# Order of work at the front of an adaLN block, and one VectorE operation moved between two others

## The chip, the cores and the metric

The kernel runs on one core of a Trainium2 chip. The metric is the device time of one execution in microseconds (us), as the median of several runs. The engines of the core have short names: PE is TensorE, DVE is VectorE, ACT is ScalarE, POOL is GpSimd, and SP issues most of the fetches. Each engine has an instruction stream of its own, written out in the order of the program, and waits for the others by semaphores.

## The reference

One transformer-like block works on x of 2048 tokens by 448 channels. A vector c gives six rows of 448 by silu(c) @ w_mod: shift, scale and gate of two halves.

```python
mod = (silu(c) @ w_mod)               # sa, ca, ga, sb, cb, gb
h = layernorm(x) * (1 + ca) + sa
x = x + ga * A(h)                     # linear attention, 16 heads of 28
h = layernorm(x) * (1 + cb) + sb
x = x + gb * B(h)                     # token-mixing MLP, 2048 -> 1792 -> 2048 over tokens

def A(h):
    q, k, v = split_heads(h @ wqkv)
    pq, pk = phi(q), phi(k)           # phi(t) = (t + 1 if t > 0 else exp(t)) + 1e-6
    kv, z = sum_s pk * v, sum_s pk
    return ((pq @ kv) / (pq @ z + 1e-6)) @ wo

def B(h):
    return (gelu(layernorm(h).T @ w1 + b1) @ w2 + b2).T
```

All data are 32-bit floats.

## The kernel before

Tokens are worked on in 16 tiles of 128. The 448 channels are cut in four chunks of 128, 128, 128 and 64. To keep the accuracy, an operand of a matrix product is split into a high part (a rounded copy that ACT writes) and a low part (the rest, which DVE or POOL writes as operand minus high part); three products of high and low parts take the place of one. Names follow that: `hh`, `hl` are the high and low parts of x transposed, `wh`, `wl` those of a projection, `pth`, `ptl` those of phi(q) transposed. The fourth chunk has 64 rows, and its low part is put into partitions 64 to 127 of the same tile as the high part.

**The front.** The projection Wk (`raw_w[1, ch]`, shown as `wr`) is scaled row by row with 1 + ca. That scale is computed in place: `col_sum(1, ch)` on DVE (line 222) multiplies a chunk of w_mod (`wt`) with a row that PE has spread over all partitions (`scr`), sums along the row, and leaves a column. Then `w_high` on ACT (line 264) scales the chunk of Wk and rounds it, and `w_low` on DVE (line 276) writes the rest. `col_sum(0, ch)` does the same for the shift sa, from which `row_part`, `row_sum` and `row_bias` make a bias row. The mean of the first layernorm is taken off after the projection: the statistics of a pair of tiles (mean and the two roots of the variance, made by `a_pow` on POOL, line 356) are written as columns of a small tile by `a_rows` (a cast, line 399, and a low part, line 402), transposed by PE (`a_transpose`, line 408), copied by ACT (`a_copy`, line 411) into spare rows of `hl`, and `close` (line 443) adds mean times column sum and bias over root in one more matmul, whose other operand is `wrow`, written by `row_out` (an ACT copy and a DVE low part, line 299). The statistics come from ACT for tiles 0 and 1 and from DVE for the others (`a_stats_dve`: `first` is BATCH_NORM_STATS, line 384, `second` the aggregate, line 387, `end` the addition of epsilon and the power on POOL). Transposed x comes as its own array (`load_xt`), already laid out on the host; SP fetches it (line 131) and the chunks of w_mod (line 142) and Wk (line 149) in the order of the program.

`projects(seq, ...)` issues the matmuls of k = h Wk (`kp`, line 436) in a list's order; `in_turn(t)` is the usual list of ten for a tile t. From tile 4 on, a loop does for each tile the projection, the closing matmul, phi(k), and the outer product of phi(k) with normalised x (`a_outer`, line 548).

**The middle** (b stage). A loop of 16 + 5 steps i works as a pipeline over tiles. In step i PE transposes the scaled phi(q) of tile i (`b_transpose`, line 848, result `tq`), multiplies the one of tile i - 1 with the joint matrix of kv and wo (`b_out`, line 878, and `b_out_last`, line 885, for the fourth chunk), computes q for a coming tile and adds the contribution of tile i - 5 to the MLP's first product (`step`, lines 935 to 937). DVE, in the order of the program, adds the residual (`b_res`, line 894), makes the denominator of tile i + 1, normalises, writes the low part of tile i (`b_low`, line 863), takes the reciprocal of the denominator (`b_recip`, line 831), writes the low parts of the fourth chunks (`b_low_last`, line 870) and scales phi(q) of tile i + 1 (`b_scale`, line 835, result `pn`); then comes the low part of the normalised tile i - 4 (`b_low2`, line 932, `h2l`). The fourth chunks of tiles i - 1 and i are transposed together when i is odd, so `b_low_last` writes two tiles then and nothing when i is even. One of its two operations reads partitions 64 to 127 and writes 0 to 63, the other does the reverse.

After that stage the MLP's two products follow, the second by a fast scheme of seven products for eight. The change doesn't touch them.

The order of instructions on every engine is the order in which the Python program calls these functions; nothing reorders them. The tiles' places in memory are given out from pools in that order too.

Of the kernel before, what the change touches and what calls it, by code (L numbers as in the profile page):

```python
# [8 lines left out]
F32 = mybir.dt.float32  # L9
# [5 lines left out]
P = 128  # L15
# [37 lines left out]
def block_kernel(ctx: ExitStack, tc: tile.TileContext, x, xt, wqkv, wo, w1, b1, w2, b2, c, wmod, wfirst, out):  # L53
# [75 lines left out]
    def load_xt(t):  # L129
        XT[t] = slot(f"xt{t}", 512)  # L130
        nc.sync.dma_start(XT[t], xt[t])
# [24 lines left out]
    for ch in range(1, 4):  # L156
        load_first(1, ch)
        load_qkv(1, chs=(ch,))
        if ch == 1:
            load_xt(1)  # L160
    load_xt(2)
    load_x(0)
    for ch in range(4):
# [53 lines left out]
    def col_sum(j, ch):  # L217
        if j not in col:
            col[j] = cst.tile([P, 4], F32, name=f"col{j}")
        p = slice(0, 64 if j == 0 and ch == 3 else P)  # L220
        w = wt.pop((j, ch))[p]
        nc.vector.scalar_tensor_tensor(w, w, 1.0, scr[p, :D + 1], op0=ALU.mult, op1=ALU.mult,
                                       accum_out=col[j][p, ch:ch + 1])
# [38 lines left out]
    def w_high(j, ch):  # L262
        Whi[j, ch] = moving(tslot, f"wh{j}_{ch}")
        nc.scalar.activation(Whi[j, ch], raw_w[j, ch], AF.Identity, scale=col[1][:, ch:ch + 1])
# [5 lines left out]
    def w_low(j, ch):  # L270
        w, r = Whi[j, ch], raw_w[j, ch]
        p = slice(0, P) if ch < 3 else slice(64, P)
        if ch < 3:
            Wlo[j, ch] = moving(tslot, f"wl{j}_{ch}")
        out = Wlo[j, ch] if ch < 3 else w[p]
        nc.vector.scalar_tensor_tensor(out, r[p], col[1][p, ch:ch + 1], w[p].bitcast(F32),
                                       op0=ALU.mult, op1=ALU.subtract)
# [119 lines left out]
    def a_rows(t):  # L397
        g, r = groups.pop(t)[:, :, 0:2], rowst[t // 2 % RING].rearrange("p (t b c) -> p t b c", t=2, b=2)
        nc.vector.tensor_copy(r[:, :, :, 0:2], g.unsqueeze(2).to_broadcast([P, 2, 2, 2]))

        def low():
            nc.vector.tensor_sub(r[:, :, 0, 2:4], g, r[:, :, 0, 0:2].bitcast(F32))
        return low
# [9 lines left out]
    def a_split_high(t):  # L413
        heads[t] = (slot(f"hh{t}", 512, F32R), slot(f"hl{t}", 512, F32R))
        nc.scalar.activation(heads[t][0], XT[t], AF.Copy)
# [12 lines left out]
    def projects(seq, j, name):  # L428
        for t, kind, ch in seq:
            hh, hl = heads[t]  # L430
            first = (t, j) not in pps
            if first:
                pps[t, j] = bank(f"{name}{t}")
            w = Wlo[j, ch] if kind == "wl" else Whi[j, ch]
            a = hl if kind == "hl" else hh
            nc.tensor.matmul(pps[t, j][:, :D], a[:, ch * P:(ch + 1) * P], w, start=first, stop=False)  # L436
# [102 lines left out]
    def a_outer(t):  # L539
# [10 lines left out]
        if t < 2:  # L550
            for ch in range(4):
# [8 lines left out]
    w_high(1, 0)  # L560
    w_low(1, 0)
    w_high(1, 1)
    a_split_high(1)
    col_sum(1, 2)
    w_low(1, 1)
    w_high(1, 2)
    col_sum(1, 3)
    w_low(1, 2)
    w_high(1, 3)
    a_split_low(1)  # L570
    w_low(1, 3)
    a_split(2)
    projects([(0, "hh", 0), (0, "hl", 0), (0, "wl", 0), (0, "hh", 1), (0, "hl", 1), (1, "hh", 0), (1, "wl", 0),
              (1, "hh", 1), (0, "wl", 1), (1, "wl", 1), (0, "hh", 2), (0, "hl", 2), (1, "hh", 2), (0, "wl", 2),
              (1, "wl", 2), (1, "hl", 0), (1, "hl", 1), (1, "hl", 2), (0, "hh", 3), (1, "hh", 3)], 1, "kp")

    def in_turn(t):
        return [(t, kind, ch) for ch in range(3) for kind in ("hh", "wl")] + [(t, "hh", 3)] + \
# [17 lines left out]
    projects(in_turn(3)[4:], 1, "kp")  # L596
    a_split_high(4)
    a_split_high(5)
    low = a_rows(0)
    first23, second23, end23 = a_stats_dve((2, 3))  # L600
    first23(0)
    low()
    first23(1)
    second23(0)
    second23(1)
    end23()
    row_out(1)
    a_split_low(4)
    a_transpose(0)
    a_copy(0)  # L610
    a_copy(1)
    a_norm(0)
    a_split_low(5)
    projects(in_turn(4)[:3], 1, "kp")
    kps = [close(t, 1) for t in (0, 1)]
    projects(in_turn(4)[3:], 1, "kp")
    load_xt(9)
    load_x(9)
    load_mod(2)
# [6 lines left out]
    low()  # L626
    a_pk(0, kps[0])
    a_low(0)
    a_transpose(2)
    projects(in_turn(5), 1, "kp")  # L630
    first45, second45, end45 = a_stats_dve((4, 5))
    first45(0)
    first45(1)
# [228 lines left out]
        hi, lo = phs[t]  # L862
        nc.vector.tensor_sub(lo, tps[t][:, :384], hi[:, :384].bitcast(F32))

    def b_low_last(t):
        ps = tps.pop(t)
        if t % 2:
            for i, s, o in ((t - 1, slice(64, P), slice(0, 64)), (t, slice(0, 64), slice(64, P))):
                hi = phs[i][0]
                nc.vector.tensor_sub(hi[o, 384:], ps[s, 384:], hi[s, 384:].bitcast(F32))  # L870

    def b_out(t):
        ph, pl = phs[t]
# [98 lines left out]
    for i in range(NT + LAG):  # L972
        if i == NT - 4:
            load_mod(5)
        if NT - 3 <= i <= NT:
            mod_part(5, i - NT + 3)
        if i == NT:
            mod_split(5)
        if i % 2 == 0 and 0 < i <= NT:
            b_out_last(i - 2)  # L980
        if i < NT:
            b_transpose(i)
        if 0 <= i - 1 < NT:
            b_out(i - 1)
        nq = min(len(late), QS.get(i, 1))
        for _ in range(nq):
            a_q(late.pop(0))
        t = i - LAG
        if t >= 0:
            if t == 0:  # L990
                accs = [bank(f"up{f}") for f in range(4)]
            if i > NT:
                if not early:
                    early = [bank(f"up{W1G[1][0] + f}") for f in range(W1G[1][1])]
                r = i - NT - 1
                step(W1G[1][0], r, early, H2h[r], H2l[r])
            step(0, t, accs, H2h[t], H2l[t])
        if i == NT:
            mp = mod_sum2(5)
            mod_out(5, mp)  # L1000
        if i < NT:
            b_high(i)
            if i % 2 == 0:
                b_beside(i)
        a_exp_q(nq)
        scale, res, norm1, norm2 = i + 1 < NT, 0 <= i - 2 < NT, 0 <= i - 3 < NT, 0 <= i - 4 < NT
        if res and i < NT + 1:
            b_res(i - 2)
        if scale:
            b_prod(i + 1)  # L1010
        if norm2:
            b_norm2(i - 4, i)
        if res:
            b_mean1(i - 2, i)
        if norm1:
            b_norm1_a(i - 3)
        if scale:
            b_sum(i + 1)
        if norm1:
            b_norm1_b(i - 3, i)  # L1020
        if scale:
            b_eps(i + 1)
        if i < NT:
            b_low(i)
        if norm1:
            b_mean2(i - 3, i)
        split_end()
        if scale:
            b_recip(i + 1)
        if i < NT:  # L1030
            b_low_last(i)
        if scale:
            b_scale(i + 1)
        if i == NT:
            b_res(i - 1)
        if norm2:
            b_low2(i - 4)
        if i == 0:
            for ch in range(4):
                wp_split(ch)  # L1040
        a_phi_q(nq)
        load_to(max(14 + (i + 1) // 2, 12 + max(0, i - 6) + max(0, i - 14)))
        if res or norm1:
            b_rstd(i, 0 if res else 1, 2 if norm1 else 1)
        split_to(8 + max(0, i - 5))
# [315 lines left out]
```

## Time and profile before

| | us |
|---|---|
| median of 3 runs | 435.99 (435.96 to 436.09) |
| the profiled execution | 435.97 |
| its span, first to last instruction | 434.3 |
| PE busy | 428.0 |
| DVE busy | 362.4 |
| ACT busy | 278.7 |
| POOL busy | 118.6 |

The profile's page gives busy times, groups of instructions and waits of one execution. A row of the timeline has the start in us from the span's start, the duration in us, the engine, the line of the kernel, the operation, what is written and read, the shape, and in brackets how long the engine stood idle before it and what ended that. A matmul's busy time is modelled and overlaps its neighbours, so the distance from one start to the next is the better measure of PE's pace; undisturbed, that distance is 0.20 us for a matmul of 448 columns here.

### The profile page before, as it was taken

To read this page: it belongs to the slowest core of one execution; us is meant where nothing else is said; L and a number is where in the kernel's file an instruction comes from. 1 tells how busy PE (TensorE), PEld (TensorE's weight loads), DVE (VectorE), ACT (ScalarE), POOL (GpSimd) and SP (SyncE) were. 2 spreads that over 40 slices of the span, in tenths; PEclk is the share of its full clock that TensorE was granted. 3 is DMA by queue.
4 is the path that set the end of the run, shared out by engine and by line. 5 is a ranking of instruction groups with operands and counts; after the bars stand their busy time and mean duration, and the time that the engine had idled before them with its cause. 6 is when DMAs were issued, how large, how long until landed. Compare 5 with 4: busy or idle time off the path is not lost.

```text
span 434.3 us, 7208 instructions
## 1 busy us (share of the span) xinstructions
PE 428.0 (99%) x2333; PEld 395.3 (91%) x2333; DVE 362.4 (83%) x813; ACT 278.7 (64%) x595; POOL 118.6 (27%) x198
## 2 busy tenths in 40 slices
PE   8999999999999999999999999999999999999996
PEld 7688899999799989989999999999999999999996
DVE  4899987689799999996679695739798998898893
ACT  5799868658568799985855273537464664645550
POOL 4335443200025477765200000010113131132010
PEclk9999999999999999999999999999999999999999
DMA  8998996564300036345427461587469987885430
GB/s 285 383 331 166 241 248 160 108 222 167 87 1 0 26 72 149 73 97 122 146 85 230 154 211 50 163 211 203 84 183 213 205 181 153 215 183 118 82 54 32
DMA packets 63941, 66.14 MB, mean 152 GB/s; under 512 B 4960, under 2 KB 55456, under 8 KB 63904
## 3 DMA queue, kind: packets, MB, share of 16 engines
q1 hardware_dynamic: 54832, 50.90, 37.5%
q0 software_dynamic: 8784, 14.32, 20.9%
q10 hardware_dynamic: 288, 0.46, 0.4%
q8 instruction: 18, 0.29, 0.3%
q14 instruction: 19, 0.16, 0.1%
HBM read 46.30 MB, written 7.34 MB: 124 GB/s over the span
## 4 chain that ended last, share of the span: by engine, by line
PE 92%; DVE 4%; DMA 2%; issue 1%; POOL 0%; ACT 0%; SPq 0%; DVEq 0%
PE y L1156 19%; PE up L935 10%; PE up L937 10%; PE up L936 10%; PE y L1157 9%; PE cacc L548 8%; PE qp L436 7%; PE op L878 6%; PE kp L436 5%; PE tq L848 1%; PE op L885 1%; DMA wr<-in_qkv_dram 1%; PE kp L443 1%; DMA xt<-in_xt_dram 1%; PE qp L443 1%; PE kvb L802 1%
## 5 line engine op out<-in xcount | busy, mean ns | idle before, releaser
L935 PE MATMUL up<-h2h,ph 128*128 128x448 f32 x224 | 81.3, 363 | 0.0
L937 PE MATMUL up<-h2h,pl 128*128 128x448 f32 x224 | 81.2, 362 | 0.0
L936 PE MATMUL up<-h2l,ph 128*128 128x448 f32 x224 | 80.8, 361 | 0.0
L1111 POOL DMA_DIRECT2D a<-a x16 | 14.1, 953 | 138.7 <-DMA a<-in_B_w_dram 77.5
L937 PEld LDWEIGHTS up<-h2h,pl 128*128 128x128 f32 x224 | 42.0, 188 | 3.2
L936 PEld LDWEIGHTS up<-h2l,ph 128*128 128x128 f32 x224 | 41.9, 187 | 3.2 <-DVE h2l L932 0.3
L935 PEld LDWEIGHTS up<-h2h,ph 128*128 128x128 f32 x224 | 42.0, 188 | 2.2
L85 DVE TENSOR_TENSOR pl<-pr,ph 128x512 fp32r<-128x512 f32 x46 | 30.8, 687 | 4.1 <-ACT ph L84 3.3
L1162 ACT ACTIVATE cc<-y 128x448 f32<-128x448 f32 x24 | 13.0, 545 | 26.9 <-PE y L1157 26.9
L84 ACT ACTIVATE ph<-pr 128x512 fp32r<-128x512 f32 x46 | 27.6, 622 | 0.8 <-PE up L937 0.5
L1075 DVE TENSOR_TENSOR u<-u,mod 128x448 f32<-128x448 f32 x14 | 8.7, 622 | 21.7 <-ACT u L1074 21.5
L1074 ACT ACTIVATE u<-up,b1c 128x448 f32<-128x448 f32 x14 | 8.7, 624 | 24.1 <-PE up L937 23.5
L436 PE MATMUL kp<-wh,hh 128*128 128x448 f32 x64 | 24.0, 380 | 0.0
L548 PE MATMUL cacc<-pkh,xh 128*128 128x448 f32 x64 | 23.6, 369 | 0.0
L1176 POOL DMA_DIRECT2D out_dram<-yt x14 | 12.7, 908 | 39.9 <-DVE yt L1167 30.6
L436 PE MATMUL qp<-wh,hh 128*128 128x448 f32 x64 | 23.4, 366 | 0.0
L828 POOL TENSOR_SCALAR den<-den 128x16 f32<-128x16 f32 x16 | 8.8, 548 | 45.3 <-DVE den L825 45.3
L548 PE MATMUL cacc<-pkl,xh 128*128 128x448 f32 x56 | 20.3, 362 | 0.0
L878 PE MATMUL op<-wph,pth 128*128 128x448 f32 x48 | 18.7, 389 | 0.0
L1117 DVE TENSOR_TENSOR a<-a,s 128x512 f32<-128x512 f32 (+1 forms) x32 | 18.5, 619 | 0.0
L84 ACT ACTIVATE s2h<-s 128x512 fp32r<-128x512 f32 (+1 forms) x16 | 8.3, 569 | 15.5 <-DVE s L1117 15.5
L1156 PE MATMUL y<-ub,a11h 128*128 128x448 f32 x56 | 18.2, 375 | 0.0
(239 smaller groups left out, 1376.4 us busy)
## 6 DMA issues: line engine op xcount, KB each, us to landing
pr<-in_B_w_dram SPq DMA_DIRECT2D x56, 256.0 KB, 3.0
a<-in_B_w_dram SPq DMA_DIRECT2D x32, 256.0 KB, 4.5
a<-in_B_w_dram SPq DMA_DIRECT2D x32, 192.0 KB, 4.5
xt<-in_xt_dram SPq DMA_DIRECT2D x16, 256.0 KB, 5.0
x<-in_A_x_dram SPq DMA_DIRECT2D x16, 224.0 KB, 5.0
wm<-in_B_wmod_dram SPq DMA_DIRECT2D x16, 196.0 KB, 5.0
out_dram<-x SPq DMA_DIRECT2D x14, 224.0 KB, 2.2
out_dram<-yt POOLq DMA_DIRECT2D x14, 224.0 KB, 5.4
```

The source lines that it names most:

```text
L84: nc.scalar.activation(hi, full, AF.Copy)
L85: nc.vector.tensor_sub(lo, full, hi.bitcast(F32))
L436: nc.tensor.matmul(pps[t, j][:, :D], a[:, ch * P:(ch + 1) * P], w, start=first, stop=False)
L548: nc.tensor.matmul(cacc[ch][:, :D], a[:, s], b, start=(t == 0 and i == 0), stop=(t == NT - 1 and i == len(todo) - 1))
L878: nc.tensor.matmul(opb[t][:, :D], a, b, start=(ch == n == 0), stop=False)
L935: nc.tensor.matmul(ps[:, :D], hi[:, sl], mh, start=first, stop=False)
L936: nc.tensor.matmul(ps[:, :D], hi[:, sl], ml, start=False, stop=False)
L937: nc.tensor.matmul(ps[:, :D], lo[:, sl], mh, start=False, stop=last)
L1111: nc.gpsimd.dma_start(w, a, accum_op=ALU.add)
L1117: nc.vector.tensor_tensor(w, raw2[q, a][i], raw2[q, b][i], op=op)
L1156: nc.tensor.matmul(ps[:, :D], h[:, s], w, start=opens and r == 0, stop=False, skip_group_check=True)
L1157: nc.tensor.matmul(ps[:, :HD], l[:, s], wh, start=False, stop=closes and r == PAIRS - 1, skip_group_check=True)
```

## The change

It has five edits.

1. The fetch of transposed x of tile 1 is issued behind chunks 2 and 3 of the scale's weights and of Wk, instead of ahead of them.
2. In the preparation of Wk, the low part of chunk 1 goes ahead of the column sum of chunk 2, the low part of chunk 2 ahead of the column sum of chunk 3, and the high part of tile 1 follows chunk 2's high part. PE's list for tiles 0 and 1 is reordered: tile 0 by chunks (high-high, low of x, low of W), then tile 1.
3. The statistics of tile 2 go ahead of the rows of tiles 0 and 1; the low parts of these rows and `row_out(1)` go ahead of the statistics of tile 3.
4. On PE, one more matmul of tile 4 goes ahead of the closing matmuls of tiles 0 and 1, and three matmuls of tile 5 ahead of the second transpose of rows.
5. In odd steps of the b stage, `b_low_last` is cut in two: the low part for tile i - 1 stays between the reciprocal and `b_scale`, the one for tile i goes behind `b_scale`.

```diff
     for ch in range(1, 4):
         load_first(1, ch)
         load_qkv(1, chs=(ch,))
-        if ch == 1:
-            load_xt(1)
+    load_xt(1)
     load_xt(2)
...
     w_high(1, 0)
     w_low(1, 0)
     w_high(1, 1)
+    w_low(1, 1)
+    col_sum(1, 2)
+    w_high(1, 2)
+    w_low(1, 2)
+    col_sum(1, 3)
     a_split_high(1)
-    col_sum(1, 2)
-    w_low(1, 1)
-    w_high(1, 2)
-    col_sum(1, 3)
-    w_low(1, 2)
     w_high(1, 3)
     a_split_low(1)
     w_low(1, 3)
     a_split(2)
-    projects([(0, "hh", 0), (0, "hl", 0), (0, "wl", 0), (0, "hh", 1), (0, "hl", 1), (1, "hh", 0), (1, "wl", 0),
-              (1, "hh", 1), (0, "wl", 1), (1, "wl", 1), (0, "hh", 2), (0, "hl", 2), (1, "hh", 2), (0, "wl", 2),
-              (1, "wl", 2), (1, "hl", 0), (1, "hl", 1), (1, "hl", 2), (0, "hh", 3), (1, "hh", 3)], 1, "kp")
+    projects([(0, kind, ch) for ch in range(3) for kind in ("hh", "hl", "wl")] +
+             [(1, kind, ch) for ch in range(3) for kind in ("hh", "wl")] +
+             [(1, "hl", ch) for ch in range(3)] + [(0, "hh", 3), (1, "hh", 3)], 1, "kp")
...
-    low = a_rows(0)
     first23, second23, end23 = a_stats_dve((2, 3))
     first23(0)
+    low = a_rows(0)
     low()
+    row_out(1)
     first23(1)
     second23(0)
     second23(1)
     end23()
-    row_out(1)
...
-    projects(in_turn(4)[:3], 1, "kp")
+    projects(in_turn(4)[:4], 1, "kp")
     kps = [close(t, 1) for t in (0, 1)]
-    projects(in_turn(4)[3:], 1, "kp")
+    projects(in_turn(4)[4:], 1, "kp")
...
+    projects(in_turn(5)[:3], 1, "kp")
     a_transpose(2)
-    projects(in_turn(5), 1, "kp")
+    projects(in_turn(5)[3:], 1, "kp")
...
-    def b_low_last(t):
-        ps = tps.pop(t)
-        if t % 2:
-            for i, s, o in ((t - 1, slice(64, P), slice(0, 64)), (t, slice(0, 64), slice(64, P))):
-                hi = phs[i][0]
-                nc.vector.tensor_sub(hi[o, 384:], ps[s, 384:], hi[s, 384:].bitcast(F32))
+    def b_low_last(t, i):
+        s, o = (slice(0, 64), slice(64, P))[::1 if i == t else -1]
+        hi = phs[i][0]
+        nc.vector.tensor_sub(hi[o, 384:], tps[t][s, 384:], hi[s, 384:].bitcast(F32))
...
         if scale:
             b_recip(i + 1)
-        if i < NT:
-            b_low_last(i)
+        if i < NT and i % 2:
+            b_low_last(i, i - 1)
         if scale:
             b_scale(i + 1)
+        if i < NT and i % 2:
+            b_low_last(i, i)
```

## The prediction

> **What bounds the kernel now.** I read the page first (busy time), then the waits of TensorE, then the engines in order of time at the front (0 to 43 us), where four of the five edits lie, and from 145 to 192 us, where the fifth lies.
>
> ```profile
> PE 428.0 (99%) x2333; PEld 395.3 (91%) x2333; DVE 362.4 (83%) x813; ACT 278.7 (64%) x595; POOL 118.6 (27%) x198
> ...
> PE kp L443 <- DVE wrow L299: 0.8, 1, 0.8
> ...
> PE tq L848 <- DVE pn L835: 0.2, 1, 0.2
> ```
>
> PE is busy for 428.0 of 434.3 us. It waits for others nowhere for long; the two waits shown are the longest after its very first instruction and the last of the list, and the edits touch both. So the change can win only about what PE stands still, and can lose whatever it makes PE wait. The stretches where DVE has no spare time decide which (columns: us, then busy PE, PEld, DVE, ACT, POOL, the granted clock, DMA):
>
> ```profile
> 18.50:34.00 15.50, 14.50 (x72) 12.29 (x71) 15.13 (x43) 13.04 (x28) 5.28 (x6) 1.00 1.03 326
> 146.00:191.50 45.50, 45.23 (x239) 41.33 (x237) 44.95 (x110) 41.53 (x95) 32.59 (x60) 1.00 0.41 88
> ```
>
> DVE is busy for 15.13 of 15.50 us and for 44.95 of 45.50 us. In both stretches PE and DVE run in step, and a stall of PE that is taken away comes back at the next thing that PE needs from DVE. So I follow DVE's order of work.
>
> **Edits 1 and 2: the fetch of xt1, and the order of the scale and Wk.** Before, in order of time on DVE and ACT (start, duration), and last a piece of the chain that ended last, the fetch of chunk 3 of Wk:
>
> ```profile
> 8.45 0.62 DVE L222 SCALAR_TENSOR_TENSOR wt<-wt,scr 128x449 f32<-128x449 f32 x1 [0.62 <-DMA wt<-in_first_dram]
> 8.99 0.68 DVE L276 SCALAR_TENSOR_TENSOR wl<-wr,col,wh 128x448 fp32r<-128x448 f32 x1
> 9.67 0.62 DVE L222 SCALAR_TENSOR_TENSOR wt<-wt,scr 128x449 f32<-128x449 f32 x1
> 10.22 0.68 DVE L276 SCALAR_TENSOR_TENSOR wl<-wr,col,wh 128x448 fp32r<-128x448 f32 x1
> 10.81 0.69 DVE L419 TENSOR_TENSOR hl<-xt,hh 128x512 fp32r<-128x512 f32 x1
> 11.54 0.69 DVE L276 SCALAR_TENSOR_TENSOR wh<-wr,col,wh 64x448 fp32r<-64x448 f32 x1
> ...
> 6.44 1.37 ACT L264 ACTIVATE wh<-wr,col 128x448 fp32r<-128x448 f32 x2 [1.01 <-DVE wt L222]
> 9.11 0.67 ACT L264 ACTIVATE wh<-wr,col 128x448 fp32r<-128x448 f32 x1 [0.70 <-DVE wt L222]
> 10.34 0.67 ACT L264 ACTIVATE wh<-wr,col 128x448 fp32r<-128x448 f32 x1 [0.56 <-DVE wt L222]
> ...
> 4.79 5.36 DMA wr<-in_qkv_dram
> ```
>
> DVE works strictly in its order: the high part of chunk 1 was ready at 6.44 + 1.37 = 7.81, yet its low part ran at 8.99, behind the sum at 8.45 that waited for its fetch. After the change the low part of chunk 1 goes first, at 7.84. The fetches of chunks 2 and 3 lose one 256 KB transfer ahead of them and land about 0.65 us sooner, but the sum of chunk 2 now starts behind that low part, at 7.84 + 0.60 = 8.44 (the step from 10.22 to 10.81): as before. Its high part on ACT stays at 9.11, ends at 9.78, and the low part of chunk 2 comes at 9.81. The sum of chunk 3 used to run in between, at 9.67; now it is queued behind that low part and starts at 10.40, the fourth high part at 11.06 instead of 10.34, and the fourth low part at 11.06 + 0.67 + 0.03 = 11.76 instead of 11.54. xt1 takes the place of the last wr, which landed at 4.79 + 5.36 = 10.15, so its high part is done at about 10.8 and its low part fits at 10.97, ahead of 11.76. **Cost: 0.22 us on DVE**, with no idle time on DVE to absorb it up to 17 us. On ACT the later fourth high part pushes everything behind it by 0.7 us, the sums over x of tiles 0 and 1, the high part and so POOL's low part of tile 2, and the high part of tile 3. DVE reads those sums late enough; PE gets tile 3 some 0.5 us later, which I estimate to bring it to the first row transpose at about 19.5. On SP's queue nothing behind xt1 moves, since the bytes ahead are the same. PE's reordered list holds the same 20 matmuls: it waits longer for chunk 2's high part and then runs through, as the parts of Wk hold it in either order.
>
> **Edits 3 and 4: rows, statistics, closing matmuls.**
>
> ```profile
> 17.13 1.41 POOL L356 TENSOR_TENSOR mv<-ve,roots 128x4 f32<-128x4 f32 x1 [3.76 <-DVE ve L371]
> 20.38 1.01 POOL L356 TENSOR_TENSOR mv<-ve,roots 128x4 f32<-128x4 f32 x1 [1.83 <-DVE ve L390]
> 39.52 1.56 POOL L356 TENSOR_TENSOR mv<-ve,roots 128x4 f32<-128x4 f32 x1 [0.33 <-DVE ve L390]
> ...
> 18.58 0.17 DVE L399 CAST rowst<-mv 128x8 fp32r<-128x8 f32 x1 [0.93 <-POOL mv L356]
> 18.66 0.62 DVE L384 BATCH_NORM_STATS2 st<-x 128x6 f32<-128x448 f32 x1
> 19.20 0.15 DVE L402 TENSOR_TENSOR rowst<-mv,rowst 128x4 fp32r<-128x4 f32 x1
> 20.13 0.17 DVE L390 TENSOR_SCALAR ve<-mv 128x4 f32<-128x4 f32 x1
> 20.33 0.63 DVE L299 TENSOR_TENSOR wrow<-rowb,wrow 2x448 fp32r<-2x448 f32 x1
> 20.99 0.69 DVE L419 TENSOR_TENSOR hl<-xt,hh 128x512 fp32r<-128x512 f32 x1
> ...
> 21.11 0.65 PE L443 MATMUL kp<-wrow,hl 98*128 98x448 f32 x2 [0.76 <-DVE wrow L299]
> ```
>
> DVE idles for 0.93 us until the power on POOL is done. The first statistics (0.54 us from start to start) move into that idle time. The power now ends at 18.54 + 0.22 = 18.76 and the cast starts at 18.79; the low rows, which need the cast, follow at 18.99, wrow at 19.18, the second statistics at 19.84, the pair of aggregates at 20.37, ve at 20.71, the next low part at 20.79 instead of 20.99. **Gain on DVE: 0.20 us**, all that is left of 0.54 after the 0.22 and 0.12 of waits between short dependent steps. wrow is done at 19.81 instead of 20.96. PE, coming at 19.5, does transpose and four matmuls (0.2 us each) and closes at about 20.45 instead of 21.11, with one matmul more behind it: 0.86 ahead. Three matmuls of tile 5 now precede the second transpose, so PE waits little there. But PE needs DVE's parts again and again, and twice it stood waiting for one (weight loads):
>
> ```profile
> 30.68 0.19 PEld L548 LDWEIGHTS cacc<-pkh,xl 128*128 128x128 f32 x1 [0.25 <-DVE xl L506]
> 37.91 0.19 PEld L436 LDWEIGHTS kp<-wh,hl 128*128 128x128 f32 x1 [0.28 <-DVE hl L419]
> ```
>
> There its lead shrinks to DVE's, 0.20 us. Bounds, by the three rows of the power: with 1.01 us for it the gain is 0.60, with 1.56 it is 0.05. I take 0.20, since the row of this very instance (1.41) is nearest.
>
> **Edit 5: the scaled tile of phi(q) between two low parts.**
>
> ```profile
> 145.93 0.62 DVE L894 SCALAR_TENSOR_TENSOR x<-op,x 128x448 f32<-128x448 f32 x1 [0.96 <-PE op L885]
> 154.38 0.24 DVE L831 RECIPROCAL den<-den 128x16 f32<-128x16 f32 x1
> 154.66 0.61 DVE L870 TENSOR_TENSOR pth<-tq,pth 64x128 fp32r<-64x128 f32 x2
> 155.29 0.62 DVE L835 SCALAR_TENSOR_TENSOR pn<-pq,den 128x448 f32<-128x448 f32 x1
> 155.84 0.62 DVE L932 TENSOR_TENSOR h2l<-y,h2h 128x448 fp32r<-128x448 f32 x1
> 175.65 0.62 DVE L932 TENSOR_TENSOR h2l<-y,h2h 128x448 fp32r<-128x448 f32 x1
> 176.28 0.62 DVE L894 SCALAR_TENSOR_TENSOR x<-op,x 128x448 f32<-128x448 f32 x1
> 190.69 0.63 DVE L835 SCALAR_TENSOR_TENSOR pn<-pq,den 128x448 f32<-128x448 f32 x1
> ...
> 156.07 0.52 PE L848 MATMUL tq<-ident,pn 128*128 128x128 f32 x3 [0.17 <-DVE pn L835]
> 191.01 0.37 PE L937 MATMUL up<-h2h,pl 128*128 128x448 f32 x1
> 191.47 0.63 PE L848 MATMUL tq<-ident,pn 128*128 128x128 f32 x4
> ```
>
> In odd steps pn comes 0.31 sooner, so the stall before the transposes at 156.07 goes. But the steps are not free to trade places. A full-height operation lets the next start 0.55 us after it began (155.29 to 155.84), 0.07 before it ends. Around the two pth, which move data between partitions 0 and 64, each starts only when the one before is done: 154.66, 154.98, 155.29. The same is seen with the fourth low part of Wk (partitions 64 on), 0.73 us after an operation of 0.69, and with wrow (96 on), 0.20 after one of 0.17. Before: 0.28 + 0.61 + 0.02 + 0.55 = 1.46 us from reciprocal to h2l. After: 0.28 + 0.32 + 0.65 (pn to its end, since a pth follows) + 0.32 = 1.57. **Cost: 0.11 us in each odd step.** DVE waits for PE at 145.93 (0.96 us idle) and from there to 191.3 practically never again; the pairs between are four (odd steps 7, 9, 11, 13), so 0.44 us. Of DVE's own waits about 0.11 go (0.09 at 176.28, 0.02 at the step before), as PE is earlier there. So the last pn ends 0.33 later than 190.69 + 0.63 = 191.32. PE already waits for that one (0.46 from 191.01 to 191.47, where 0.20 is usual), so **the last lock gives +0.33 us**, and what PE won at 156 is gone. Bounds: if the changed neighbours cost nothing, -0.11; if each pair costs as much again, +0.75. I take +0.33.
>
> The Trainium skill, page VectorE: DVE Perf Modes, section Two Vector instructions with no wait between them, says that an instruction whose inputs or output start in another quadrant of 32 partitions than the last ones waits until all earlier ones are done. By it the new order has four such instructions (pth, pn, pth, h2l), the old three (pth, pth, pn), and the 0.44 us stands; if instead the two pth only wait for one another, parting them frees both, and the sum of this edit is rival A's -0.11.
>
> **The sum.** DVE's wait at 145.93 shows PE leading there, so the front's lead passes whole: -0.20 + 0.33 = +0.13 us. The profiled execution took 435.97 us (span 434.3), the median of the runs is 435.99: forecast **436.1 us**, no change to speak of. Its own range is 435.7 to 436.5.
>
> **Rivals.**
> A. The neighbours of the pth don't hold DVE: -0.20 - 0.11, 435.7 us. For it: the two pth work on one PSUM tile, so they may wait for each other only; against: the other pairs above, which share nothing.
> B. Faster: DVE does not hold PE. PE keeps 0.86 at the front and the stalls before the transposes (0.3 at 156.07 and about as much in those after): about 1.4 less, 434.6 us. It decides if DVE's parts come more than 0.9 us ahead of PE's need after 30 us. Against: the two weight loads that waited; for: DVE idles 0.93 us right at the place.
> C. Slower: the clock. PE's longest pause among its first matmuls grows to an estimated 1.0 us, from chunk 1's last matmul near 8.6 to chunk 2's first at 9.8.
>
> ```profile
> 1.11 2.93 PE L186 MATMUL warm<-ones 128*128 128x128 f32 x12 [1.11 <-DVE roots L106]
> 5.60 1.83 PE L186 MATMUL warm<-ones 128*128 128x128 f32 x14
> ```
>
> The first twelve took 0.24 us each, the later fourteen 0.13. If PE falls back for as long as that first stretch, it loses 2.93 x 0.46 = 1.4 us; its lead of 0.8 at the second transpose becomes a lag of 0.6, in place of the 0.20 gained: 0.6 + 0.33 = +0.93, 436.9 us. It decides from 1.3 us of lost clock. Against: the granted clock is 1.00 in both stretches above.
> The Trainium skill, page TensorE: Matmul & The Clock Gate, section Part 1, has the clock halved only after an idle window of about 3.4 us; by that rule a pause of 1.0 us costs nothing.
>
> **How the numbers follow.** Forecast 0.60, A 0.16, B 0.12, C 0.12. 0.2% is 0.87 us, about what a measurement of this kernel can tell from no change; so B is faster (0.12), C and the forecast's upper tail slower (0.13), the rest no change (0.75). The range leaves out B and some of C's upper part: 435.2 (the front's best, 0.60, with A's -0.11 and a little) to 436.9.
>
> **What would show it.** Right: the fourth low part of Wk near 11.8, wrow done near 19.8, the closing matmuls near 20.4, the weight loads for xl and hl of tile 8 only 0.2 sooner; odd steps 0.11 longer on DVE, the last transposes near 191.6. Wrong: closing matmuls after 21; PE still 0.8 ahead at 38 us; h2l 0.54 after a pth pair's end or no longer odd steps; a clock under 1.00 before 20 us.

## The result, and the profile after

The changed kernel takes 436.73 us (median of 22 runs, 436.16 to 437.06) beside 436.07 us for the kernel before on the same chip (22 runs, 435.84 to 436.41), 0.66 us more. The ratio is 1.0013, with an interval of 1.0007 to 1.0019. The ratio, here and below, comes from all executions but three far above the rest (467.76 us in e2, 1503.98 in e9, and 1504.07 of the kernel before beside e5, e9 and e10), so it need not be the quotient of the two medians. The result is inside the predicted range (435.2 to 436.9) and within 0.2%, but above the forecast's own range (435.7 to 436.5) and more than the +0.13 us of the sum. The profiled execution of the changed kernel took 436.21 us (span 434.5), only 0.24 us more than the profiled one of before. So there are two questions: did the steps go as predicted in the profiled execution, and why does the median lose more than that execution?

The page of the changed kernel, its first part (busy time) and two rows of its waits:

```profile
PE 428.4 (99%) x2333; PEld 395.0 (91%) x2333; DVE 363.1 (84%) x813; ACT 278.3 (64%) x595; POOL 118.0 (27%) x198
...
PE kp L435 <- ACT wh L263: 0.8, 1, 0.8
...
PE tq L848 <- DVE pn L835: 0.5, 1, 0.5
```

The wait for `wrow` (0.8 us before) is gone from PE's list, and a wait for a high part of Wk has come. PE's wait for `pn` is 0.5 instead of 0.2, and it is another one (the last of the stage, below). Busy time by stretch of the changed kernel (columns as in the prediction):

```profile
18.50:34.00 15.50, 15.50 (x75) 12.92 (x74) 14.72 (x44) 13.13 (x28) 6.05 (x7) 1.00 1.05 325
146.00:191.50 45.50, 45.18 (x237) 40.84 (x235) 44.83 (x109) 40.95 (x95) 32.78 (x59) 1.00 0.40 88
```

In the first stretch PE is now busy throughout (15.50 us, 14.50 before). That full microsecond is not in the time. The timeline of the changed kernel at the front, DVE first, then PE and its weight loads:

```profile
5.98 0.62 DVE L221 SCALAR_TENSOR_TENSOR wt<-wt,scr 128x449 f32<-128x449 f32 x1 [2.01 <-PE scr L210]
...
8.54 0.62 DVE L221 SCALAR_TENSOR_TENSOR wt<-wt,scr 128x449 f32<-128x449 f32 x1
9.90 0.69 DVE L275 SCALAR_TENSOR_TENSOR wl<-wr,col,wh 128x448 fp32r<-128x448 f32 x1 [0.74 <-ACT wh L263]
11.87 0.68 DVE L275 SCALAR_TENSOR_TENSOR wh<-wr,col,wh 64x448 fp32r<-64x448 f32 x1
18.91 0.17 DVE L398 CAST rowst<-mv 128x8 fp32r<-128x8 f32 x1 [0.40 <-POOL mv L355]
19.32 0.63 DVE L298 TENSOR_TENSOR wrow<-rowb,wrow 2x448 fp32r<-2x448 f32 x1
20.94 0.68 DVE L418 TENSOR_TENSOR hl<-xt,hh 128x512 fp32r<-128x512 f32 x1
...
8.80 0.36 PE L435 MATMUL kp<-wl,hh 128*128 128x448 f32 x1
9.92 0.47 PE L435 MATMUL kp<-wh,hh 128*128 128x448 f32 x1 [0.76 <-ACT wh L263]
20.60 0.57 PE L442 MATMUL kp<-wrow,hl 98*128 98x448 f32 x2
30.62 0.19 PEld L547 LDWEIGHTS cacc<-pkh,xl 128*128 128x128 f32 x1 [0.34 <-DVE xl L505]
37.85 0.19 PEld L435 LDWEIGHTS kp<-wh,hl 128*128 128x128 f32 x1 [0.26 <-DVE hl L418]
```

The fourth low part of Wk starts at 11.87 (11.54 before), DVE waits 0.40 us instead of 0.93 for the power, `wrow` is started at 19.32 instead of 20.33 and the closing matmuls at 20.60 instead of 21.11. Yet the low part of tile 4 comes at 20.94 instead of 20.99, and the two weight loads that wait for DVE come 0.06 sooner: PE's lead of half a microsecond has shrunk to DVE's few hundredths. The timeline of the changed kernel in the middle, an odd step on DVE and the end of the stage on PE:

```profile
145.83 0.62 DVE L892 SCALAR_TENSOR_TENSOR x<-op,x 128x448 f32<-128x448 f32 x1 [0.83 <-PE op L883]
154.28 0.24 DVE L831 RECIPROCAL den<-den 128x16 f32<-128x16 f32 x1
154.55 0.29 DVE L868 TENSOR_TENSOR pth<-tq,pth 64x128 fp32r<-64x128 f32 x1
154.87 0.63 DVE L835 SCALAR_TENSOR_TENSOR pn<-pq,den 128x448 f32<-128x448 f32 x1
155.53 0.28 DVE L868 TENSOR_TENSOR pth<-tq,pth 64x128 fp32r<-64x128 f32 x1
155.85 0.63 DVE L930 TENSOR_TENSOR h2l<-y,h2h 128x448 fp32r<-128x448 f32 x1
...
190.84 0.36 PE L935 MATMUL up<-h2h,pl 128*128 128x448 f32 x1
191.73 0.63 PE L848 MATMUL tq<-ident,pn 128*128 128x128 f32 x4 [0.53 <-DVE pn L835]
```

From the reciprocal to `h2l` it is now 155.85 - 154.28 = 1.57 us, 1.46 before. The last transposes start 0.89 us after the matmul ahead of them (0.46 before) and 45.90 us after the residual at 145.83; before, that distance was 191.47 - 145.93 = 45.54 us.

### The profile page after: what moved, and what is told of

Its sections match the earlier page's. It is cut to its first block, busy times and chain, and to the rows that moved or that the text cites. A ratio compares the mean times of both kernels' runs of the same rounds, so it can differ in the third digit from the quotient of the medians.

```text
span 434.5 us, 7209 instructions
## 1 busy us (share of the span) xinstructions
PE 428.4 (99%) x2333; PEld 395.0 (91%) x2333; DVE 363.1 (84%) x813; ACT 278.3 (64%) x595; POOL 118.0 (27%) x198
## 4 chain that ended last, share of the span: by engine, by line
PE 85%; DVE 10%; DMA 2%; issue 1%; ACT 1%; SPq 0%; DVEq 0%
PE y L1156 19%; PE y L1157 9%; PE up L934 9%; PE up L933 9%; PE up L935 9%; PE cacc L547 8%; PE qp L435 7%; PE kp L435 6%; PE op L876 3%; DMA xt<-in_xt_dram 2%; DVE y L906 1%; DVE pn L835 1%; DVE y L902 1%; DVE x L892 1%; DVE pd L821 1%
## 5 line engine op out<-in xcount | busy, mean ns | idle before, releaser
L1075 DVE TENSOR_TENSOR u<-u,mod 128x448 f32<-128x448 f32 x14 | 8.7, 621 | 21.7 <-ACT u L1074 21.5
```

## The experiments

All kernels were compared in five rounds with the kernel before on the same chip (11 executions each, 12 of e2, one of them profiled). They are told by question. Five marks of the profiled executions carry most of what follows. S is the start of the first column sum on DVE (line 221 or 222 by kernel), W that of the fourth low part of Wk, H that of the low part of tile 4 at the front, R that of the residual near 146 us, T that of the last transposes (us).

| kernel | S | W | H | R | T | span |
|---|---|---|---|---|---|---|
| before | 5.77 | 11.54 | 20.99 | 145.93 | 191.47 | 434.3 |
| changed | 5.98 | 11.87 | 20.94 | 145.83 | 191.73 | 434.5 |
| changed, again (e0) | 6.50 | 12.40 | 21.47 | 146.36 | 192.28 | 435.1 |
| e1, edits 1 to 4 | 5.80 | 11.76 | 20.82 | 145.77 | 191.33 | 434.1 |
| e2, edit 5 | 6.50 | 11.67 | 21.13 | 146.08 | 192.00 | 434.8 |
| e3, edits 3 and 4 | 6.50 | 11.46 | 20.94 | 145.90 | 191.47 | 434.3 |
| e9, the same again | 6.33 | 11.96 | 21.04 | 145.97 | 191.54 | 434.4 |
| e4, edits 1 and 2 | 6.75 | 12.64 | 22.10 | 147.01 | 192.56 | 435.3 |
| e5, both low parts behind | 6.50 | 11.54 | 21.00 | 145.96 | 191.88 | 434.7 |
| e6, another order | 6.06 | 11.09 | 21.14 | 146.08 | 191.64 | 434.4 |
| e7, before, later start | 6.51 | 11.47 | 20.93 | 145.89 | 191.43 | 434.2 |
| e8, changed, later start | 6.44 | 12.33 | 21.39 | 146.32 | 192.22 | 435.0 |
| e10, a third order | 5.83 | 10.45 | 20.66 | 145.61 | 191.16 | 433.9 |
| e11, and fetches moved | 5.63 | 10.34 | 20.88 | 145.78 | 191.34 | 434.1 |

From H to R it is 124.89 to 124.96 us in all fourteen, and from T to the end of the span 242.7 to 242.9. So two places decide the time: when DVE starts the low part of tile 4 at the front, and how long R to T takes. R to T is 45.54 to 45.57 us in the kernels with the old order of the middle, and 45.90 to 45.92 in those with edit 5 or with e5's order.

### The whole change again, the front alone, the middle alone

First, the changed kernel a second time, with nothing edited.

> The whole change once more, beside the kernel before on the same chip, since its first 22 times spread over 0.9 us (436.16 to 437.06) where those before spread over 0.6. My theory (front -0.20, scaled tile +0.33) gives +0.13 us; the first measurement gave +0.66. If the loss beyond +0.13 belongs to the kernel, it shows again, +0.5 to +0.8; if it belongs to the chip of that day, +0.1 to +0.3.

Measured: 436.40 us beside 436.07 (ratio 1.0007, 0.9999 to 1.0016), from 435.97 to 436.83. This time the profiled execution was one of the longer ones (436.81). Its R to T is 45.92, as in the first profile; what is longer lies ahead of 21.5 us. Over both measurements the 33 executions of the changed kernel have a median of 436.62, and 10 of them lie at 436.34 or below.

Then the front without edit 5 (against the changed kernel; `b_low_last` itself goes back too):

```diff
-        if i < NT and i % 2:
-            b_low_last(i, i - 1)
+        if i < NT:
+            b_low_last(i)
         if scale:
             b_scale(i + 1)
-        if i < NT and i % 2:
-            b_low_last(i, i)
```

> Edits 1 to 4 alone (the front); the b stage as before. My theory: the fourth low part of Wk some 0.2 us later, wrow done 1 us sooner, -0.20 us in the end. Rival, the front loses in most executions: +0.2 to +0.5, with a start that varies more from one execution to the next. Rival B (DVE does not hold PE): -0.8.

Measured: 435.91 beside 436.07, -0.16 us (1.0001, 0.9993 to 1.0010; 435.58 to 437.22). The rows of its timeline:

```profile
20.82 0.69 DVE L418 TENSOR_TENSOR hl<-xt,hh 128x512 fp32r<-128x512 f32 x1
...
145.77 0.62 DVE L894 SCALAR_TENSOR_TENSOR x<-op,x 128x448 f32<-128x448 f32 x1 [0.95 <-PE op L885]
...
191.33 0.63 PE L848 MATMUL tq<-ident,pn 128*128 128x128 f32 x4
```

The low part of tile 4 is 0.17 sooner than before, the residual 0.16, the last transposes 0.14: the front's gain is DVE's, and it reaches the end. The marks show this for one execution, which began early (S at 5.80); over all eleven the interval of the ratio does not tell the gain from nothing, and four of them took 436.46 us or more.

And edit 5 alone (against the kernel before):

```diff
-        if i < NT:
-            b_low_last(i)
+        if i < NT and i % 2:
+            b_low_last(i, i - 1)
         if scale:
             b_scale(i + 1)
+        if i < NT and i % 2:
+            b_low_last(i, i)
```

> Edit 5 alone: in odd steps the scaled tile goes between the two low parts, the front as before. My theory: four odd steps longer by 0.11 us each on DVE, the last transposes 0.33 us later, +0.33 us in the end. Rival A (the neighbours of the low parts are not held): -0.11. Rival U (the unexplained half of the loss is here): +0.8.

Measured: 436.48 beside 436.07, +0.41 us (1.0011, 1.0002 to 1.0020). R to T is 45.92, 0.38 more than in the kernel before, with this row on PE:

```profile
192.00 0.63 PE L848 MATMUL tq<-ident,pn 128*128 128x128 f32 x4 [0.54 <-DVE pn L835]
```

So the cost of edit 5 is shown by itself, in the time and at its place, and it is the predicted one.

### What in edit 5 costs it

Both low parts behind `b_scale`, with the old front (against the kernel before):

```diff
         if scale:
             b_recip(i + 1)
-        if i < NT:
-            b_low_last(i)
         if scale:
             b_scale(i + 1)
+        if i < NT:
+            b_low_last(i)
```

> The kernel before with both low parts behind the scaled tile, in odd steps: reciprocal, pn, pth, pth, h2l. My theory (an operation in another quadrant starts when all before are done, and so does the one after it): 0.28 + 0.65 + 0.32 + 0.32 = 1.57 us from reciprocal to h2l instead of 1.46, the last transposes 0.3 later, +0.3 us. Rival A (the two pth wait only for one another): 1.35 to 1.40 us, -0.1.

Measured: 436.41 beside 436.12, +0.29 us (1.0007, 0.9998 to 1.0016). Its odd step on DVE:

```profile
154.41 0.24 DVE L831 RECIPROCAL den<-den 128x16 f32<-128x16 f32 x1
154.68 0.63 DVE L835 SCALAR_TENSOR_TENSOR pn<-pq,den 128x448 f32<-128x448 f32 x1
155.34 0.61 DVE L870 TENSOR_TENSOR pth<-tq,pth 64x128 fp32r<-64x128 f32 x2
155.98 0.63 DVE L932 TENSOR_TENSOR h2l<-y,h2h 128x448 fp32r<-128x448 f32 x1
```

The two `pth` are neighbours again, and the step still takes 1.57 us. What costs is that `pn`, which used to let `h2l` start 0.07 us ahead of its own end, now has a half-height operation behind it and runs to its end: 0.66 us to the next start instead of 0.55, which is all of the 0.11. The two `pth` themselves take 0.64 us to the next start, 0.63 in the kernel before. Whether one `pth` or both stand behind `pn` makes no difference. Rival A needed 1.35 to 1.40 here, and falls.

### Rows alone, Wk alone

Edits 3 and 4 without the new fetch and order of Wk (against the kernel before):

```diff
-    low = a_rows(0)
     first23, second23, end23 = a_stats_dve((2, 3))
     first23(0)
+    low = a_rows(0)
     low()
+    row_out(1)
     first23(1)
     second23(0)
     second23(1)
     end23()
-    row_out(1)
...
-    projects(in_turn(4)[:3], 1, "kp")
+    projects(in_turn(4)[:4], 1, "kp")
     kps = [close(t, 1) for t in (0, 1)]
-    projects(in_turn(4)[3:], 1, "kp")
+    projects(in_turn(4)[4:], 1, "kp")
...
+    projects(in_turn(5)[:3], 1, "kp")
     a_transpose(2)
-    projects(in_turn(5), 1, "kp")
+    projects(in_turn(5)[3:], 1, "kp")
```

> Edits 3 and 4 alone: statistics, rows and closing matmuls in the new order, the fetch of xt1 and the order of Wk as before. My theory: the 0.22 us that edits 1 and 2 cost DVE are gone, so -0.42 us. If edits 1 and 2 cost nothing: -0.20. If PE is not held by DVE: -0.8 or more.

Measured: 435.64 beside 436.07, -0.43 us (0.9993, 0.9985 to 1.0002). The same kernel once more, on another chip:

> Edits 3 and 4 alone once more, to see whether they are faster than the kernel before by more than the spread: -0.3 to -0.5 us again, if the first result was no accident; 0 to -0.1 otherwise.

Measured: 436.06 beside 436.12, -0.06 us (0.9997, 0.9988 to 1.0006). The gain of the first measurement was not repeated; over the 21 other executions of the two, without the one of 1503.98 us, the median is 435.79. The marks say more than the medians. From W to H it is 9.45 or 9.46 us in every kernel with the old order of rows (before, e2, e4, e5, e7) and 9.06 to 9.08 in the changed kernel, e0, e1, e8 and e9: 0.39 us, the predicted 0.42 of the rows. In the profile of e3 the gain is missing (9.48), and one row shows why:

```profile
19.32 0.63 DVE L299 TENSOR_TENSOR wrow<-rowb,wrow 2x448 fp32r<-2x448 f32 x1 [0.45 <-ACT wrow L298]
```

There DVE comes to `wrow` earlier than ACT has written its high part. ACT in turn had waited 0.48 us for the bias row (`rowb`) of PE, which started the last two matmuls of that row at 17.80 instead of 17.01 us: this execution began late (S at 6.50). So with edits 3 and 4 a late start can take their gain through PE and ACT, even where the old order of Wk keeps W in place.

Edits 1 and 2 alone (against the kernel before; the long list of PE is the one in the change):

```diff
-        if ch == 1:
-            load_xt(1)
+    load_xt(1)
...
-    a_split_high(1)
-    col_sum(1, 2)
     w_low(1, 1)
+    col_sum(1, 2)
     w_high(1, 2)
-    col_sum(1, 3)
     w_low(1, 2)
+    col_sum(1, 3)
+    a_split_high(1)
```

> Edits 1 and 2 alone: the fetch of xt1 behind all chunks, and the new order of the preparation of Wk. My first theory: +0.22 us in every execution. New theory, from the traces so far: in some executions the warming matmuls of PE run slowly for longer (fourteen in 3.4 us instead of 1.8), the row that PE spreads for the scale comes about 0.5 us later, and only the new order has no idle time on DVE to take that up; so +0.2 us in some executions and +0.7 in others, median between, and a wider spread than the kernel before.

Measured: 436.30 beside 436.12, +0.18 us (1.0009, 1.0000 to 1.0018). Six of the eleven executions lie between 436.18 and 436.30, the others between 436.47 and 437.13; the profiled one is of the latter (437.08), and its fourth low part starts at 12.64, 0.77 later than in the changed kernel's first profile.

### When DVE begins

The marks S and W show what the medians hide. With the new order of Wk, W comes 5.89 to 5.96 us after S, for S from 5.80 to 6.75 (changed, e0, e1, e4, e8). With the old order it comes between 11.46 and 11.67 in five profiles (before, e2, e3, e5, e7) although S lies anywhere from 5.77 to 6.51; only in e9, where the fetch of chunk 2 landed later, is it 11.96. And S differs between executions, mostly since PE starts slowly for a longer or shorter while. The spread of the row (`scr`), for which the first column sum waits, in the kernel before:

```profile
3.86 1.50 PE L209 MATMUL scr<-ident,sc 112*128 112x112 f32 x8
```

The same spread, the fourteen warm-up matmuls behind it and that column sum in the second profile of the changed kernel:

```profile
3.86 2.02 PE L208 MATMUL scr<-ident,sc 112*128 112x112 f32 x8
6.33 3.36 PE L185 MATMUL warm<-ones 128*128 128x128 f32 x14
...
6.50 0.62 DVE L221 SCALAR_TENSOR_TENSOR wt<-wt,scr 128x449 f32<-128x449 f32 x1 [2.78 <-PE scr L210]
12.40 0.69 DVE L275 SCALAR_TENSOR_TENSOR wh<-wr,col,wh 64x448 fp32r<-64x448 f32 x1
```

The spread takes 2.02 us instead of 1.50 from the same start, the fourteen behind it 3.36 us (0.24 each) where the kernel before took 1.83 (0.13 each), and S is at 6.50 instead of 5.77. The same start with the old order of Wk, in the profile of edit 5 alone:

```profile
6.32 3.36 PE L186 MATMUL warm<-ones 128*128 128x128 f32 x14
...
6.50 0.62 DVE L222 SCALAR_TENSOR_TENSOR wt<-wt,scr 128x449 f32<-128x449 f32 x1 [2.78 <-POOL hl L419]
11.67 0.69 DVE L276 SCALAR_TENSOR_TENSOR wh<-wr,col,wh 64x448 fp32r<-64x448 f32 x1
```

The view names POOL at this sum, but its start is that of the second profile of the changed kernel, and so are PE's rows. S is 0.73 later than in the kernel before, W only 0.13. To test this I made DVE begin later by two more rounds of the first warm-up, in both kernels.

```diff
-WARM = 6
+WARM = 8
```

> The kernel before, with eight warming matmuls ahead of the spread row instead of six, so that the row comes later in every execution, about 0.6 us. New theory: the wait of DVE for the fetch of chunk 2 (0.62 us idle) takes it up, the fourth low part of Wk stays near 11.6, and the time stays within 0.15 us of before. Rival (a later row delays either order alike): +0.5.

> The whole change, with eight warming matmuls instead of six. New theory: nothing takes up the later row, the fourth low part of Wk comes near 12.4, and the time is +0.7 to +0.9 us against before, with little spread left. Rival (the wide spread comes from elsewhere): +0.4 as measured for the whole change, and the spread stays.

Measured, on one chip: the kernel before with the later start 436.47 beside 436.12, +0.35 us (1.0009, 1.0001 to 1.0018; 435.96 to 437.43); the changed kernel with it 437.04, +0.92 us (1.0022, 1.0013 to 1.0031; 436.35 to 437.50). The rows of the kernel before with the later start, and behind them those of the changed one:

```profile
6.51 0.62 DVE L222 SCALAR_TENSOR_TENSOR wt<-wt,scr 128x449 f32<-128x449 f32 x1 [2.78 <-PE scr L211]
11.47 0.69 DVE L276 SCALAR_TENSOR_TENSOR wh<-wr,col,wh 64x448 fp32r<-64x448 f32 x1
```

```profile
6.44 0.62 DVE L221 SCALAR_TENSOR_TENSOR wt<-wt,scr 128x449 f32<-128x449 f32 x1 [2.47 <-PE scr L210]
12.33 0.68 DVE L275 SCALAR_TENSOR_TENSOR wh<-wr,col,wh 64x448 fp32r<-64x448 f32 x1
```

In the profiled executions the kernel before swallows 0.74 us of delay (435.96 us beside 435.97); the changed one passes on the 0.46 that S is later (W +0.46, H +0.45) and takes 436.76 beside 436.21. That is what the theory says. But 435.96 is the fastest of that kernel's eleven executions, and by the medians the theory is not borne out: the later start costs the kernel before 0.35 us and the changed one about as much (437.04 against 436.62 over its 33 executions), which is nearer to the rival of the first of these two runs. I take it that in the other executions S came later still and the 0.62 us of room was used up, but those are not profiled, and the spread of the changed kernel did not shrink either. That the old order absorbs a late start is shown in single executions (e2, e3, e5, e7); what it does to the medians stays open.

### Two other orders of the front

If DVE's room for a late start was what the new order lacks, an order that keeps room and the rows' gain should win. Both are edits 1, 3 and 4 with another order of Wk, and no edit 5. In the first, both sums come ahead of the low part of chunk 2 (against the changed kernel, its order of Wk alone):

```diff
     w_low(1, 1)
     col_sum(1, 2)
     w_high(1, 2)
-    w_low(1, 2)
     col_sum(1, 3)
-    a_split_high(1)
     w_high(1, 3)
-    a_split_low(1)
+    w_low(1, 2)
+    a_split_high(1)
     w_low(1, 3)
+    a_split_low(1)
```

> Edits 1, 3 and 4, no edit 5, and another order for Wk: both column sums of chunks 2 and 3 ahead of the low part of chunk 2, and the fourth low part ahead of the low part of xt1. My theory: DVE no longer waits 0.7 us for a high part, the fourth low part of Wk starts near 10.5 instead of 11.54, the next sum waits for its fetch near 12.1, and a late start of PE finds room; -0.5 us against before, and -0.1 against the run with edits 3 and 4 alone. If that room is worth nothing: -0.4, as that run.

Measured: 435.96 beside 436.12, -0.16 us (0.9997, 0.9988 to 1.0006; 435.38 to 436.45). W is at 11.09, but the low part of tile 1, which used to stand ahead of it, now stands between it and the next sums, and these begin at 12.43 instead of the 12.25 of before. S was 0.29 later, and from S to these sums it is 6.37 us, 6.48 before, still with waits of 0.35 and 0.20 us on DVE. So a W moved forward in this way is nearly no gain, and the -0.5 us that I expected was a miss.

In the second, the sum of chunk 2 also goes ahead of the low part of chunk 1 (against e6):

```diff
-    w_low(1, 1)
     col_sum(1, 2)
+    w_low(1, 1)
     w_high(1, 2)
```

> Edits 1, 3 and 4 with a third order for Wk: column sum of chunk 2, low part of chunk 1, column sum of chunk 3, low parts of chunks 2 and 3, and xt1's parts last. DVE then waits for nothing between 8 and 12 us. Theory: the sums for sa start at 12.1, bound by their fetch, whether PE's row comes early or late; -0.5 us, 0.1 below the run with edits 3 and 4 alone, with less spread than the order tried before (both column sums first). Rival (DVE's own work from the first column sum on is what sets that time, so a late row still costs): -0.2, as the order tried before.

Measured: 435.75 beside 436.12, -0.37 us (0.9992, 0.9984 to 1.0001), with the smallest spread of the kernels tried, 435.64 to 436.25. Its rows on DVE:

```profile
10.45 0.69 DVE L275 SCALAR_TENSOR_TENSOR wh<-wr,col,wh 64x448 fp32r<-64x448 f32 x1
...
12.24 0.62 DVE L221 SCALAR_TENSOR_TENSOR wt<-wt,scr 128x449 f32<-128x449 f32 x1 [0.38 <-DMA wt<-in_first_dram]
...
20.66 0.68 DVE L418 TENSOR_TENSOR hl<-xt,hh 128x512 fp32r<-128x512 f32 x1
```

W has come forward by 1.09 us, and the next sum starts 0.01 us sooner than before: DVE now stands waiting for the fetch of the shift's first chunk. That wait is room that a late start could use; this execution began early (S at 5.83), so no profile shows it used. The gain at H, 0.33 us, is the rows'. By the ratio this is the best version I measured, if only just (0.9993 in the first measurement of e3); its interval still touches 1.

So I moved the fetches of the shift's first two chunks ahead (against e10):

```diff
     load_xt(1)
+    load_first(0, 0)
     load_xt(2)
+    load_first(0, 1)
     load_x(0)
-    for ch in range(4):
-        if ch == 2:
-            load_x(1)
-        load_first(0, ch)
+    load_x(1)
+    load_first(0, 2)
+    load_first(0, 3)
```

> The third order for Wk with edits 1, 3 and 4, and the first two chunks of the shift's weights fetched ahead of xt2 and of x of tile 0. The run before it showed DVE idle for 0.38 us there, waiting for the first of these fetches. Theory (DVE sets the pace of the front until 43 us): that time is won too, -0.7 us against before. Rival (the sums over x of tiles 0 and 1 on ACT, whose fetch is now later, or PE set the pace by then): -0.4, as the run before it.

Measured: 436.08 beside 436.07, no change (1.0000, 0.9991 to 1.0010): a miss. Its rows, of DVE and POOL:

```profile
11.66 0.62 DVE L222 SCALAR_TENSOR_TENSOR wt<-wt,scr 128x449 f32<-128x449 f32 x1
12.76 1.10 DVE L282 TENSOR_SCALAR accb<-wr,col 128x448 f32<-128x448 f32 x1
19.26 0.63 DVE L299 TENSOR_TENSOR wrow<-rowb,wrow 2x448 fp32r<-2x448 f32 x1 [0.24 <-ACT wrow L298]
...
12.32 1.29 POOL L419 TENSOR_TENSOR hl<-xt,hh 128x512 fp32r<-128x512 f32 x1 [5.83 <-ACT hh L415]
```

The sums did start 0.58 sooner. But the column's first use (`accb`), 0.45 us in the other kernels, falls beside POOL's low part of tile 2 and takes 1.10, and later `wrow` waits for ACT: H is at 20.88, 0.22 behind e10's. What the fetches won was given back at these two places.

## Why the prediction was right, and what it mis-sized

**What bounds the kernel.** Right, and more strictly than I had argued. PE led by half a microsecond at the closing matmuls (20.60 instead of 21.11), and of that 0.10 was left at R, where DVE's low part at H was 0.05 sooner; H to R is the same 124.9 us in fourteen profiles. Rival B, by which PE keeps its lead, needed R about as much sooner, and falls.

**Edits 3 and 4.** Forecast -0.42 on DVE, measured -0.39 from W to H. The stall of PE at `wrow` went, as said.

**Edit 5.** Forecast 1.46 to 1.57 us in each odd step; measured 1.57, with each of its four parts within 0.01. Forecast +0.33 at the last lock, measured +0.36 to +0.38 from R to T. The stall at 156 went (the transposes start at 155.65 without a wait) and came back at the end of the stage, where PE waits 0.53 us for the last `pn`. By the page VectorE: DVE Perf Modes of the Trainium skill, section Two Vector instructions with no wait between them, the operation behind `pn` waits for all earlier ones in the new order and in e5, and not in the order before. The traces agree: 0.66 us from `pn` to the next start in both, 0.55 before. The number of operations that wait is not what costs: by the same rule of the Trainium skill e5 has three of them, as many as the order before, and takes 1.57 us like the four of the new order.

**Edits 1 and 2.** This is the mis-sized term: "Cost: 0.22 us on DVE". From S to W the cost was 0.12 to 0.19 us (5.89 to 5.96 instead of 5.77), a little less than that. But I took the start S from one profiled execution as a constant. The order before has 0.62 us of waiting at the sum of chunk 2, which I quoted and used only as time that the low part could fill. It was also what absorbed a late start. With it gone, the delay of S, up to 0.98 us in these profiles, goes to W and from there to the end; the old order let through 0.13 of it or less, but where the fetch was late. In the first profile of the changed kernel S was 0.21 late, in the second 0.73, and the whole execution was 0.6 us longer. That gives the parts of the profiled execution's span: +0.21 for S, +0.12 from S to W, -0.38 from W to H, -0.05 from H to R, +0.36 from R to T, -0.06 behind T, together +0.20 (434.3 to 434.5). Without the start that is -0.01; with the parts as measured alone, -0.17 for the front (e1's T less its S) and +0.38 for edit 5 (e2), it is +0.21. So the start would have to account for some 0.3 to 0.55 of the +0.55 us of the 33 executions' median. That step is inferred and not shown: only one execution of each measurement is profiled, and by the medians of e7 and e8 a later start costs both kernels about alike. By the ratios, which take in all executions, the parts do add up: 1.0001 for the front (e1) and 1.0011 for edit 5 (e2) beside 1.0013 and 1.0007 for the whole. So edit 5 accounts for the loss as forecast, and what did not come, over many executions, is the front's 0.20 us.

**Rival C, the clock.** As I put it, it did not happen: PE paused for 1.12 us (8.80 to 9.92), and behind it two matmuls start 0.20 us apart (10.96 and 11.16), the undisturbed pace. But the pace of PE did cost time, at another place: before the pause, by the moment at which the first matmuls become fast. The page TensorE: Matmul & The Clock Gate of the Trainium skill, section Part 1, says that the activity window runs freely and that the transition depends on where in it a kernel's first matmul lands, within 500 ns either way. The 1.83 and 3.36 us of the same fourteen matmuls agree that it moves, but here it moves by some 4 us (fast from 5.80 us in one profile, slow until 9.69 in the other).

**Luck.** That 436.73 us lies in the predicted range is in part luck. It is above the forecast's own 436.5, and the room above that was left for rival C, whose pause cost nothing.

**What stays open.** The share of executions with a late start, for either kernel, and with it the loss of the median beyond edit 5. The smaller 0.2 us by which S is late in the changed kernel's first profile is not PE's pace. It comes from the first of three small operations on DVE ahead of the spread; the first row is of the kernel before, the second of the changed one:

```profile
2.70 0.61 DVE L194 TENSOR_SCALAR ec<-ec 128x4 f32<-128x4 f32 x1 [1.61 <-ACT ec L192]
...
2.77 0.78 DVE L193 TENSOR_SCALAR ec<-ec 128x4 f32<-128x4 f32 x1 [1.69 <-ACT ec L191]
```

With it the three operations end 0.25 us later, and the spread starts at 4.11 us instead of 3.86. They end that late in five of the eight profiles with the fetch order of edit 1 (changed, e4, e6, e8, e11) and in none of the other six; whether edit 1 is the cause, no run tests.

## What to carry to other kernels

An engine's wait for a fetch is not only idle time; it may be the buffer between a start that varies and a chain that does not forgive. Before filling it, look at how the first instructions of that engine differ between executions, and compare many executions, not one profile with one profile. And where two engines run in step, find a mark of the engine that leads the chain (here one low part at 21 us) and read every edit by how that mark moves: stalls taken from the other engine show up again at the next lock.

## What the runs showed of the hardware that I had not expected

- PE's first matmuls change from 0.24 to 0.13 us each at a moment that differs by some 4 us between two executions of the same kernel: in one the fourteen at 5.80 us are fast already (1.83 us), in the other they are slow until 6.33 + 3.36 = 9.69. The granted clock reads 1.00 there in both.
- An operation of DVE with one tensor input, `accb` of 128x448, took 1.10 instead of 0.45 us in e11, where POOL ran a tensor operation of 1.29 us beside it; in one profile only, so the cause is not shown.
- On DVE a half-height operation that moves data between partitions 0 and 64 takes its overlap from the full-height one ahead of it: 0.66 us from one start to the next instead of 0.55. That is the 0.11 us per odd step, and it is the same if two of them stand together behind the full-height one (1.57 us in both).
